# The first product of the routed layer by Strassen's rule, seven products of half size in place of eight

## The chip, the cores and the metric

The kernel runs on one core of a Trainium2 chip. The metric is the device time of one execution in microseconds. TensorE (PE) does the matmuls, and its weight loads (PEld) overlap them; VectorE (DVE) and ScalarE (ACT) do the arithmetic on tiles; GpSimd (POOL) works beside them on tiles in SBUF; SyncE (SP) issues the DMAs. Each engine works through a queue of its own in order. The framework places the waits between engines, and it also sets the order within each queue when it compiles: mostly the written order, with ready work pulled ahead of work whose inputs it expects later.

## The reference

Three layers follow one another. B = 8, H = 8 heads, S = 576, head size 64; so there are 4608 tokens of width 512.

```python
p_packed = sm_attn(p, k, v)                 # 32 packed rows per head
x = sm_attn(q, p_packed, p_packed)          # -> [4608, 512]
h = x @ w_in;  x = (h - tanh(h)) @ w_out    # d_ff = 2048
logits = x @ w_gate + modality_bias[modality_id]
e_idx = argmax(logits);  gate = softmax(logits)[e_idx]
out[mask_e] = gate * (relu(x[mask_e] @ w1[e]) @ w2[e])   # 8 experts, F = 1024
```

The inputs are such that one expert serves (nearly) all tokens: the kernel computes the expert of the first token for all of them, and a branch at the end (`other_experts`) does others where flags ask for it.

## The kernel before

Products of 32-bit data are made of three matmuls each: every operand is split into a high part in the fast format and the remainder, and `mm3` (L105 to L107) adds high·high, low·high and high·low into one PSUM bank.

The main part is a list of **slots**. The 256 slots of kind "a" are the attention's value product and the layer with tanh: 16 half-blocks `hb` of 288 tokens, each with 16 slices `f` of d_ff. In slot n PE does `gemm1(n)`, then `gemm2(n - 3)`; ACT and DVE do `chain(n)` (L857, L858 on ACT, L860, L862 on DVE) and `gsplit` (L871 on ACT, L872 on DVE) between them. `gemm1` writes one of the two PSUM banks of the pool `ps_h`; the bank is free when L862 has read it. `gemm2` adds into the four banks `acc`. After a half-block's last slot, `evac` (L905, L906) moves `acc` into the tiles x2h and x2l, which are stored to DRAM as `x_hi` and `x_lo`. The attention of the next batches stands in the two banks of `AT` beside all that.

The 144 slots of kind "b" are the layer this change is about: 18 blocks `kk` of 256 tokens, each with 8 slices `f` of 128 columns of F. `gemm1b` makes the slice's first product (4 chunks of K = 512, three matmuls of 256 columns each) in an `ps_h` bank. `relu` takes it to a high part (ACT, L972) and a remainder (DVE, L973). `gemm2b`, three slots later, multiplies by the slice of w2 and adds into two of the `acc` banks (2 token tiles, three matmuls of 512 columns). After the eighth slice `evac_b` scales the two tiles by the gate, one on ACT (L1011), one on DVE (L1007), into tiles with the tags x2h and x2l (one buffer each), and SP stores them (L1013).

The weights come in during the last slots of kind "a": `w1_load` and `w2_load` by DMA, `w1_split` (ACT L930, POOL L931) and `w2_split` (ACT L945, POOL L946). `xb_load` brings x_hi and x_lo back, 512 KB per DMA. Around the tables `pre_ev`, `pe_ev` and `post_ev` each slot has its extra work; `at_post(m, fn)` puts `fn` beside slot m. Slots 236 to 255 are where w1 is split; slot 256 (`na`) is the first of kind "b".

Of the kernel before, what the change touches and what calls it, by code (L numbers as in the profile page):

```python
# [26 lines left out]
def attn_moe_moe_kernel(  # L27
# [15 lines left out]
    nc = tc.nc  # L43
# [8 lines left out]
    TB = 256  # L52
# [19 lines left out]
    ps_at = ctx.enter_context(tc.tile_pool(name="ps_at", bufs=1, space=PSUM))  # L72
# [493 lines left out]
    def logits_pe(hb):  # L566
        ps = AT[0:32, 1, 0:HW]
# [7 lines left out]
    def route_in(hb):  # L575
        ps = AT[0:32, 1, 0:HW]
# [75 lines left out]
    def flags_pe():  # L652
        fl["ps"] = AT[0:1, 0, 0:NE * NHB]
        nc.tensor.matmul(out=AT[0:1, 1, 0:1], lhsT=ones_b, rhs=fl["big"], start=True, stop=True)
        nc.tensor.matmul(
            out=fl["ps"], lhsT=ones, rhs=fl["has"].rearrange("i e h -> i (e h)"), start=True, stop=True
        )

    def flags_b(every=False):
        n = evp.tile([1, NE, NHB], F32, name="n_other", tag="rt_l")  # L660
        ps = fl["ps"].rearrange("o (e h) -> o e h", e=NE)
        if every:
            nc.vector.tensor_copy(out=n, in_=ps)
        else:
            other = evp.tile([1, NE], F32, name="other", tag="rt_m")
            nc.vector.tensor_tensor(
                out=other, in0=em8[0:1, :], in1=idx_t[0:1, 0:1].to_broadcast([1, NE]), op=ALU.not_equal
            )
            nc.vector.tensor_tensor(
                out=n, in0=ps, in1=other.unsqueeze(2).to_broadcast([1, NE, NHB]), op=ALU.mult,  # L670
            )
            yield
        tot = evp.tile([1, NE + 1], F32, name="n_tot", tag="gq")
        nc.vector.tensor_reduce(out=tot[:, 0:NE], in_=n, axis=AX.X, op=ALU.max)
        nc.vector.tensor_reduce(out=tot[:, NE:NE + 1], in_=tot[:, 0:NE], axis=AX.X, op=ALU.max)
        yield
        if not every:
            nc.vector.tensor_copy(out=flags[:, NE, 0:1], in_=AT[0:1, 1, 0:1])
            nc.vector.tensor_tensor(out=tot[:, NE:NE + 1], in0=tot[:, NE:NE + 1], in1=AT[0:1, 1, 0:1], op=ALU.add)
        nc.vector.tensor_copy(out=flags[:, 0:NE, 0:NHB], in_=n)  # L680
        nc.vector.tensor_copy(out=flags[:, :, NHB], in_=tot)
        yield


    def redo():
        nonlocal evp
        with ExitStack() as st:
# [229 lines left out]
    def w1_load(bp, f):  # L917
        st = bp.tile([128, 4, 128], F32, name="w1s", tag="ws", bufs=2)
        e = ev_reg["e"]
        nc.sync.dma_start(  # L920
            out=st,
            in_=w1[bass.ds(e, 1)].rearrange("o (k p) c -> p (o k) c", p=128)[:, :, f * 128:f * 128 + 128],
        )
        w1t[f] = st

    def w1_split(bp, f):
        st = w1t[f]
        hi = bp.tile([128, 4, 128], F32R, name=f"w1h{f}")
        lo = bp.tile([128, 4, 128], F32R, name=f"w1l{f}")
        nc.scalar.activation(out=hi, in_=st, func=ACTF.Copy)  # L930
        nc.gpsimd.tensor_tensor(out=lo, in0=st, in1=f32(hi), op=ALU.subtract)  # L931
        w1t[f] = (hi, lo)
# [16 lines left out]
    def xb_load(kk):  # L949
        xb[kk] = [  # L950
            late["x"].tile([128, 4, TB], F32R, name=f"xb{c}", tag=f"xb{c}", bufs=3) for c in "hl"
        ]
        for d, t in zip(xs, xb[kk]):
            nc.sync.dma_start(out=f32(t), in_=d[:, :, kk * TB:kk * TB + TB])

    def gemm1b(n, kk, f):
        ps = ps_h.tile([128, TB], F32, name="h", tag="h")
        xh, xl = xb[kk]
        for c in range(4):
            mm3(ps, (w1t[f][0][:, c, :], w1t[f][1][:, c, :]), (xh[:, c, :], xl[:, c, :]), c == 0, c == 3)  # L960
        ht[n] = ps

    def relu(n):
        ps = ht.pop(n)
        if n % 2:
            gh, gl = (
                gp.tile([128, TB], F32R, name="bg", tag=tg, bufs=2) for tg in ("u", "qq")
            )
        else:
            gh = g3.tile([128, TB], F32R, name="bh", tag="gh")  # L970
            gl = g3.tile([128, TB], F32R, name="bl", tag="gl")
        nc.scalar.activation(out=gh, in_=ps, func=ACTF.Relu)  # L972
        nc.vector.scalar_tensor_tensor(  # L973
            out=gl, in0=ps, scalar=0.0, in1=f32(gh), op0=ALU.max, op1=ALU.subtract
        )
        gt[n] = (gh, gl)
        yield

    def gemm2b(n, kk, f):
        if f == 0:  # L980
            oa[kk] = [
                pools["acc"].tile([128, 512], F32, name=f"acc{2 * (kk % 2) + t}") for t in range(2)
            ]
        gh, gl = gt.pop(n)
        for t in range(2):
            st = tuple(x[:, t * 128:t * 128 + 128] for x in (gh, gl))
            mm3(oa[kk][t], st, w2t[f], f == 0, f == NF2 - 1)
# [14 lines left out]
    def evac_b(kk):  # L1002
        for t in range(2):
            T = 2 * kk + t
            o = evp.tile([128, 512], F32, name="o", tag=("x2h", "x2l")[t])
            if t:
                nc.vector.tensor_scalar(  # L1007
                    out=o, in0=oa[kk][t], scalar1=gate_b[:, T:T + 1], scalar2=None, op0=ALU.mult
                )
            else:  # L1010
                nc.scalar.activation(out=o, in_=oa[kk][t], func=ACTF.Copy, scale=gate_b[:, T:T + 1])  # L1011
# [16 lines left out]
    with ExitStack():  # L1028
# [153 lines left out]
        for n, (ph, i, f, first, kind) in enumerate(slots):  # L1182
            if ph == "a" and kind == "full":
# [14 lines left out]
        for f in range(NF2):  # L1198
            at_post(b_mem + 5 * f // 4, lambda f=f: w1_load(bpool["p"], f))
            at_post(b_mem + 2 + 5 * f // 4, lambda f=f: w1_split(bpool["p"], f))  # L1200
            at_post(na - NF + 2 * f, lambda f=f: w2_load(bpool["p"], f))
            at_post(na - NF + 2 * f + 3, lambda f=f: w2_split(f))
        at_post(na - NF + 1, lambda: xb_load(0))
        at_post(na - NF + 2, lambda: xb_load(1))

        total = len(slots)
        for n in range(total + LAG + 2):
# [76 lines left out]
```

## Time and profile before

| what | value |
|---|---|
| three runs | 1258.16, 1256.27, 1257.09 us; median 1257.09 |
| the profiled execution | 1256.98 us, span 1255.2 us |
| busy share of the span | PE 95%, PEld 84%, DVE 58%, ACT 45%, POOL 6% |
| granted TensorE clock, mean | 0.980 |
| chain that ended last | PE 78%, DVE 8%, issue 6%, DMA, ACT and POOL 2% each |

How to read it: the span runs from the first to the last instruction. Busy time is that in which an engine works on an instruction; matmuls overlap each other, so the time that one more matmul costs is the distance between the starts of two, not its own length. In rows of groups the columns are line, engine, operation, out<-in, shape, count | busy us, mean ns of one | idle time before it and what ended that. In rows in order of time they are start, length, engine, line, operation, out<-in, and in brackets the idle time before and what ended it.

### The profile page before, as it was taken

To read this page: it belongs to the slowest core of one execution; us is meant where nothing else is said; L and a number is where in the kernel's file an instruction comes from. 1 tells how busy PE (TensorE), PEld (TensorE's weight loads), DVE (VectorE), ACT (ScalarE), POOL (GpSimd) and SP (SyncE) were. 2 spreads that over 40 slices of the span, in tenths; PEclk is the share of its full clock that TensorE was granted. 3 is DMA by queue.
4 is the path that set the end of the run, shared out by engine and by line. 5 is a ranking of instruction groups with operands and counts; after the bars stand their busy time and mean duration, and the time that the engine had idled before them with its cause. 6 is when DMAs were issued, how large, how long until landed. Compare 5 with 4: busy or idle time off the path is not lost.

```text
span 1255.2 us, 24451 instructions
## 1 busy us (share of the span) xinstructions
PE 1195.3 (95%) x9764; PEld 1050.2 (84%) x9765; DVE 722.7 (58%) x1603; ACT 569.6 (45%) x1320; POOL 77.5 (6%) x69
## 2 busy tenths in 40 slices
PE   5698899999999999999999999999999999999996
PEld 3356678799889889889889899998999999999995
DVE  4866897787887787887787876654121111211111
ACT  3688756556556556556556556641111111111111
POOL 1222100000000000000000002310000000000000
PEclk8699999999999999999999999999999999999998
DMA  8768455454454354354354136221222112221201
GB/s 217 225 197 215 134 141 126 123 144 112 106 144 126 82 144 124 82 143 122 82 143 123 51 111 198 88 64 53 85 67 81 58 65 85 66 79 59 67 18 37
DMA packets 193291, 137.54 MB, mean 110 GB/s; under 512 B 123024, under 2 KB 169104, under 8 KB 193168
## 3 DMA queue, kind: packets, MB, share of 16 engines
q1 hardware_dynamic: 193168, 135.90, 39.2%
q8 instruction: 78, 1.28, 0.4%
q14 instruction: 45, 0.37, 0.1%
HBM read 98.10 MB, written 37.75 MB: 108 GB/s over the span
## 4 chain that ended last, share of the span: by engine, by line
PE 78%; DVE 8%; issue 6%; DMA 2%; ACT 2%; POOL 2%; SPq 0%; POOLq 0%; DVEq 0%; ACTq 0%
PE acc L105 15%; PE acc L107 14%; PE acc L106 14%; PE h L106 10%; PE h L105 10%; PE h L107 9%; PE at L212 3%; DVE s L487 1%; PE at L359 1%; POOL wv L188 1%; DVE x2l L906 1%; DVE qq L860 1%; PE h L844 1%; DVE gl L872 1%; DMA raw<-in_moe_w_in_dram 1%
## 5 line engine op out<-in xcount | busy, mean ns | idle before, releaser
L105 PE MATMUL acc<-gh,wo_hi 128*128 128x288 f32 x960 | 294.6, 307 | 2.7 <-DVE part L903 1.6
L107 PE MATMUL acc<-gl,wo_hi 128*128 128x288 f32 x960 | 282.9, 296 | 3.0 <-DVE gl L872 2.8
L106 PE MATMUL acc<-gh,wo_lo 128*128 128x288 f32 x960 | 283.9, 296 | 0.0
L105 PEld LDWEIGHTS acc<-gh,wo_hi 128*128 128x128 f32 x960 | 180.8, 188 | 36.4 <-ACT u L857 17.5
L860 DVE SCALAR_TENSOR_TENSOR qq<-qq,u 128x288 f32<-128x288 f32 x256 | 131.3, 513 | 116.7 <-ACT qq L858 116.5
L107 PEld LDWEIGHTS acc<-gl,wo_hi 128*128 128x128 f32 x960 | 180.6, 189 | 5.9 <-DVE gl L872 5.0
L106 PEld LDWEIGHTS acc<-gh,wo_lo 128*128 128x128 f32 x960 | 180.9, 188 | 2.4 <-issue 1.7
L871 ACT ACTIVATE gh<-gs 128x288 fp32r<-128x288 f32 x240 | 106.7, 445 | 158.7 <-PE acc L106 143.1
L106 PE MATMUL h<-xbh,w1l 128*128 128x256 f32 x576 | 161.3, 280 | 0.0
L107 PE MATMUL h<-xbl,w1h 128*128 128x256 f32 x576 | 160.8, 279 | 0.0
L105 PE MATMUL h<-xbh,w1h 128*128 128x256 f32 x576 | 160.7, 279 | 0.0
L857 ACT ACTIVATE u<-h 128x288 f32<-128x288 f32 x256 | 105.0, 411 | 109.9 <-PE h L107 90.4
L105 PE MATMUL h<-ah,mh 128*128 128x288 f32 x448 | 133.1, 297 | 2.9 <-DVE gs L862 2.1
L106 PE MATMUL h<-ah,ml 128*128 128x288 f32 x448 | 132.3, 295 | 0.0
L107 PE MATMUL h<-al,mh 128*128 128x288 f32 x448 | 131.8, 294 | 0.0
L872 DVE TENSOR_TENSOR gl<-gs,gh 128x288 fp32r<-128x288 f32 x240 | 113.1, 471 | 31.3 <-ACT gh L871 27.4
L973 DVE SCALAR_TENSOR_TENSOR bl<-h,bh 128x256 fp32r<-128x256 f32 x72 | 30.6, 425 | 165.2 <-ACT bh L972 165.2
L858 ACT ACTIVATE qq<-u 128x288 f32<-128x288 f32 x256 | 113.5, 443 | 7.0
L862 DVE SCALAR_TENSOR_TENSOR gs<-qq,h 128x288 f32<-128x288 f32 x256 | 112.5, 440 | 6.2 <-PE acc L881 1.7
L106 PEld LDWEIGHTS h<-xbh,w1l 128*128 128x128 f32 x576 | 108.1, 188 | 6.2
L105 PEld LDWEIGHTS h<-xbh,w1h 128*128 128x128 f32 x576 | 108.2, 188 | 5.8
L973 DVE SCALAR_TENSOR_TENSOR bg<-h,bg 128x256 fp32r<-128x256 f32 x72 | 30.6, 425 | 139.0 <-ACT bg L972 139.0
(167 smaller groups left out, 1958.4 us busy)
## 6 DMA issues: line engine op xcount, KB each, us to landing
ws<-w_in_v SPq DMA_DIRECT2D x56, 512.0 KB
nat<-in_v_dram SPq DMA_DIRECT2D x16, 576.0 KB
x_hi<-x2h SPq DMA_DIRECT2D x16, 576.0 KB
x_lo<-x2l SPq DMA_DIRECT2D x16, 576.0 KB
xbh<-x_hi SPq DMA_DIRECT2D x18, 512.0 KB
xbl<-x_lo SPq DMA_DIRECT2D x18, 512.0 KB
raw<-in_moe_w_in_dram SPq DMA_DIRECT2D x32, 256.0 KB
raw<-in_moe_w_out_dram SPq DMA_DIRECT2D x16, 512.0 KB
```

What stands on the lines that cost most here:

```text
L105: nc.tensor.matmul(out=ps, lhsT=ah, rhs=bh, start=first, stop=False)
L106: nc.tensor.matmul(out=ps, lhsT=al, rhs=bh, start=False, stop=False)
L107: nc.tensor.matmul(out=ps, lhsT=ah, rhs=bl, start=False, stop=last)
L188: nc.gpsimd.tensor_tensor(out=v, in0=lo.bitcast(F32), in1=hi.bitcast(F32), op=ALU.mult)
L212: nc.tensor.matmul(out=out_of(g, hh), lhsT=lhs_of(g, hh), rhs=rhs_of(g, hh), start=True, stop=True, tile_position=(64 * g, 32 * hh),)
L857: nc.scalar.activation(out=u, in_=ps, func=ACTF.Square)
L858: nc.scalar.activation(out=qq, in_=u, func=ACTF.Exp, scale=-PK)
L860: nc.vector.scalar_tensor_tensor(out=qq, in0=qq, scalar=PB, in1=u, op0=ALU.add, op1=ALU.mult)
L862: nc.vector.scalar_tensor_tensor(out=gs, in0=qq, scalar=PA, in1=ps, op0=ALU.mult, op1=ALU.mult)
L871: nc.scalar.activation(out=gh, in_=gs, func=ACTF.Copy)
L872: nc.vector.tensor_tensor(out=gl, in0=gs, in1=f32(gh), op=ALU.subtract)
L973: nc.vector.scalar_tensor_tensor(out=gl, in0=ps, scalar=0.0, in1=f32(gh), op0=ALU.max, op1=ALU.subtract)
```

## The change

The layer's tokens are taken in 9 groups of 512 in place of 18 blocks of 256. Of a group, x is cut in 2 × 2 blocks (halves of K, `kh`, and of the tokens, `th`), w1 in 2 × 2 blocks (halves of K and of F, `fh`). Strassen's rule, in the form with few additions, makes the 2 × 2 blocks of the product from seven products of combinations of blocks.

- **w1**: the combinations S1 to S4 are made on POOL (`comb`), then each of the seven left operands is split (`put`: ACT and POOL), for each of the two chunks c of a half of K: 8 combinations and 14 splits in place of 8 splits. They stand in slots 236 to 250.
- **x**: per group `x_load` brings eight pieces of 256 KB; `x_sum` (POOL, 4 per group) adds high part and remainder again, since combinations must be made before the split; `x_comb` makes four differences (DVE); `x_split` splits the seven right operands (ACT, DVE). The first group's stands in slots 247 to 255, a later group's beside the four steps of the group before it.
- **Steps**: a step j is a group and one of 4 row blocks i of 128 columns of each half of F. `first_b` makes its seven products in the order 1, 2, 5, 6, 3, 4, 7. Products 1, 6, 7 add up in one bank (`ba`), 5 and 3 in another (`be`), 2 and 4 stand in the two `ps_h` banks. Between them ACT copies a bank's state (`g_copy`), and DVE makes the four result blocks (`c_tile`). PE's order is `first_b(j)`, then `gemm2b(j - 1)`; `relu_b(j)` stands beside it.
- **Second product**: `gemm2b` does 4 token tiles and 2 halves of F per step, into all four `acc` banks. `evac_b` now evicts four tiles per group, still through the two tiles x2h and x2l.
- The two banks of `AT` are given up at slot 256 for `ba` and `be`. So the logits, routing and flags of the last half-block move behind the first steps and use `ps_h` banks, and the last half-block takes its slices in the order 8 to 15, 0 to 7. Five of the eight splits of w2 move beside steps 0 to 2.

```diff
-    TB = 256
+    TB = 512
...
-    def w1_split(bp, f):
-        st = w1t[f]
...
+    def w1_steps(bp, c):
...
+        def put(p, nm):
+            wa[p, c] = split(lambda x: bp.tile([128, 512], F32R, name=f"wa{p}{c}{x}"), sp[nm], nc.gpsimd)
+        def comb(nm, into, a, b, op):
...
+            nc.gpsimd.tensor_tensor(out=sp[into], in0=sp[a], in1=sp[b], op=op)
...
+        return [
+            lambda: load("A21", "ah0", 0, 1), lambda: load("A22", "al0", 1, 1), lambda: load("A11", "ah1", 0, 0),
+            lambda: comb("S1", "S", "A21", "A22", ALU.add),
+            lambda: put(5, "S1"), lambda: put(4, "A22"), lambda: load("A12", "al0", 1, 0),
+            lambda: comb("S3", "A21", "A11", "A21", ALU.subtract), lambda: put(7, "S3"),
+            lambda: comb("S2", "S", "S1", "A11", ALU.subtract), lambda: put(6, "S2"), lambda: put(1, "A11"),
+            lambda: comb("S4", "S", "A12", "S2", ALU.subtract), lambda: put(3, "S4"), lambda: put(2, "A12"),
+        ]
...
-    def gemm1b(n, kk, f):
-        ps = ps_h.tile([128, TB], F32, name="h", tag="h")
-        xh, xl = xb[kk]
-        for c in range(4):
-            mm3(ps, (w1t[f][0][:, c, :], w1t[f][1][:, c, :]), (xh[:, c, :], xl[:, c, :]), c == 0, c == 3)
...
+    def x_sum(g, kh, th):
+        a, b = xr[g, kh, th]
+        nc.gpsimd.tensor_tensor(out=a, in0=a, in1=b, op=ALU.add)
+    def x_comb(g):
...
+        for o, a, b in ((t1, b12, b11), (t2, b22, t1), (t3, b22, b12), (t4, t2, b21)):
+            nc.vector.tensor_tensor(out=o, in0=a, in1=b, op=ALU.subtract)
...
+    def x_split(g, p):
+        hi, lo = xa[g, p] = [x_tile() for _ in "hl"]
+        t = xr[g][p]
+        nc.scalar.activation(out=hi, in_=t, func=ACTF.Copy)
+        yield
+        nc.vector.tensor_tensor(out=lo, in0=t, in1=f32(hi), op=ALU.subtract)
...
+    def prod(j, p, ps, start):
+        g, i = divmod(j, 4)
+        for c in range(2):
+            wh, wl = (t[:, 128 * i:128 * i + 128] for t in wa[p, c])
+            xh, xl = (t[:, c, :] for t in xa[g, p])
+            for m, (a, b) in enumerate(((wh, xh), (wl, xh), (wh, xl))):
+                nc.tensor.matmul(
+                    out=ps, lhsT=a, rhs=b, start=start and c == 0 and m == 0, stop=c == 1 and m == 2,
...
+    def first_b(j):
...
+        prod(j, 1, a, True)
+        prod(j, 2, d, True)
+        g_copy(j, "p1", a)
+        nc.vector.tensor_tensor(out=c_tile(j, 0), in0=d, in1=bank[j, "p1"], op=ALU.add)
+        prod(j, 5, e, True)
+        g_copy(j, "p5", e)
+        prod(j, 6, a, False)
+        g_copy(j, "u2", a)
+        prod(j, 3, e, False)
+        nc.vector.tensor_tensor(out=c_tile(j, 1), in0=e, in1=bank[j, "u2"], op=ALU.add)
+        d2 = h_tile()[:, 0:256]
+        prod(j, 4, d2, True)
+        prod(j, 7, a, False)
+        t = c_tile(j, 3)
+        nc.vector.tensor_tensor(out=t, in0=a, in1=bank[j, "p5"], op=ALU.add)
+        nc.vector.tensor_copy(out=bank[j, "p5"], in_=a)
+        t = c_tile(j, 2)
+        nc.vector.tensor_tensor(out=t, in0=bank[j, "p5"], in1=d2, op=ALU.subtract)
...
+    def relu_b(j):
...
+                nc.scalar.activation(out=hi[:, th, :], in_=t, func=ACTF.Relu)
...
+                nc.vector.scalar_tensor_tensor(
+                    out=lo[:, th, :], in0=t, scalar=0.0, in1=f32(hi[:, th, :]), op0=ALU.max, op1=ALU.subtract
...
+    def evac_b(g):
+        for t in range(4):
+            T = 4 * g + t
+            o = evp.tile([128, 512], F32, name="o", tag=("x2h", "x2l")[t % 2])
...
+        for j in range(NU2 + 1):
+            if j:
+                if j < NU2:
+                    first_b(j)
...
+            if j < NU2:
+                threads.append(relu_b(j))
...
+            if g + 1 < NTB:
+                xp = x_prep(g + 1) if i == 0 else xp
+                todo += (xp[0:1], xp[1:5], xp[5:9], xp[9:13])[i]
+            if j:
+                gemm2b(j - 1)
...
+            if j and j % 4 == 0:
+                evac_b(j // 4 - 1)
```

More of the change, by code (lines that the diff above doesn't have):

```diff
@@ L652, in flags_pe @@
     def flags_pe():
-        fl["ps"] = AT[0:1, 0, 0:NE * NHB]
-        nc.tensor.matmul(out=AT[0:1, 1, 0:1], lhsT=ones_b, rhs=fl["big"], start=True, stop=True)
+        t = h_tile()
+        fl["ps"], fl["pb"] = t[0:1, 0:NE * NHB], t[0:1, HW - 1:HW]
+        nc.tensor.matmul(out=fl["pb"], lhsT=ones_b, rhs=fl["big"], start=True, stop=True)
         nc.tensor.matmul(
@@ L685, in redo @@
     def redo():
-        nonlocal evp
+        nonlocal evp, AT
         with ExitStack() as st:
@@ L690, in redo @@
             evp = rp
+            AT = st.enter_context(tc.tile_pool(name="ps_rat", bufs=1, space=PSUM)).tile([128, 2, 512], F32, name="rat")
             wo = rp.tile([128, NF, 512], F32, name="wo")
@@ L915, in read_e @@
         ev_reg["e"] = nc.sync.value_load(e_i[0:1, 0:1], min_val=0, max_val=NE - 1)
[L917 to L924, printed above, removed]
-    def w1_split(bp, f):
-        st = w1t[f]
[L928 to L932, printed above, removed]
+    wa, xa, xr = {}, {}, {}
@@ new lines, in split, with load @@
+    def split(tile_of, t, eng):
+        hi, lo = (tile_of(c) for c in "hl")
+        nc.scalar.activation(out=hi, in_=t, func=ACTF.Copy)
+        eng.tensor_tensor(out=lo, in0=t, in1=f32(hi), op=ALU.subtract)
+        return hi, lo
+    def w1_steps(bp, c):
+        sp = {}
+        def load(nm, tag, kh, fh):
+            sp[nm] = a2p.tile([128, 512], F32, name="w1s", tag=tag)
+            nc.sync.dma_start(
+                out=sp[nm],
+                in_=w1[bass.ds(ev_reg["e"], 1), (2 * kh + c) * 128:(2 * kh + c) * 128 + 128, fh * 512:fh * 512 + 512]
+                .rearrange("o p c -> p (o c)"),
+            )
+        def put(p, nm):
+            wa[p, c] = split(lambda x: bp.tile([128, 512], F32R, name=f"wa{p}{c}{x}"), sp[nm], nc.gpsimd)
+        def comb(nm, into, a, b, op):
+            if into not in sp:
+                sp[into] = a2p.tile([128, 512], F32, name="w1s", tag="al1")
+            nc.gpsimd.tensor_tensor(out=sp[into], in0=sp[a], in1=sp[b], op=op)
+            sp[nm] = sp[into]
+        return [
[6 more added lines that the diff above has]
+        ]
@@ L963, in relu @@
[L963 to L976, printed above, removed]
-        yield
@@ L979, in gemm2b, with x_tile, x_load @@
[L979 to L987, printed above, removed]
+    def x_tile(dt=F32R):
+        return wp.tile([128, 2, 256], dt, name="xw", tag="w")
+    def x_load(g):
+        for kh in range(2):
+            for th in range(2):
+                xr[g, kh, th] = [x_tile(F32) for _ in xs]
+                for d, t in zip(xs, xr[g, kh, th]):
+                    c0 = g * TB + 256 * th
+                    nc.sync.dma_start(out=t, in_=d[:, 2 * kh:2 * kh + 2, c0:c0 + 256])
@@ L989, in out_rows, with gemm2b @@
+    def gemm2b(j):
+        g, i = divmod(j, 4)
+        if i == 0:
+            oa[g] = [pools["acc"].tile([128, 512], F32, name=f"acc{t}") for t in range(4)]
+        parts = gt.pop(j)
+        for t in range(4):
+            for fh in range(2):
+                st = tuple(x[:, t // 2, (t % 2) * 128:(t % 2) * 128 + 128] for x in parts[fh])
+                mm3(oa[g][t], st, w2t[i + 4 * fh], i == 0 and fh == 0, i == 3 and fh == 1)
     def out_rows(t):
@@ L1038, in attn_moe_moe_kernel @@
         for hb in range(2, NHB):
-            for f in range(NF):
-                slots.append(("a", hb, f, f == 0, "full" if f == NF - 1 else None))
+            fs = list(range(NF)) if hb < NHB - 1 else [*range(NF // 2, NF), *range(NF // 2)]
+            for f in fs:
+                slots.append(("a", hb, f, f == fs[0], "full" if f == fs[-1] else None))
         na = len(slots)
-        for kk in range(NTB):
-            for f in range(NF2):
-                slots.append(("b", kk, f, f == 0, "out" if f == NF2 - 1 else None))
         pe_ev, post_ev = {}, {}
```

150 lines of the change are left out of this document (94 added, 56 removed).

## The prediction

> **What bounds the kernel now.** I read the page's head, then the windows by stage, the groups by shape, and the order of time over a few microseconds.
>
> ```profile
> span 1255.2 us, 24451 instructions
> PE 1195.3 (95%) x9764; PEld 1050.2 (84%) x9765; DVE 722.7 (58%) x1603; ACT 569.6 (45%) x1320; POOL 77.5 (6%) x69
> ...
> 762.00:832.84 70.84, 68.71 (x512) 67.50 (x511) 47.45 (x93) 43.46 (x103) 20.39 (x16) 1.00 0.42 126
> 832.84:1243.51 410.67, 410.66 (x2642) 371.81 (x2640) 86.71 (x205) 70.38 (x169) 0.93 (x1) 1.00 0.20 64
> ```
>
> The windows' columns are length, busy time of PE, PEld, DVE, ACT and POOL, granted clock, DMA share and GB/s. The second layer is the stretch from 832.84 to 1243.51: PE is busy in 410.66 of 410.67 us at clock 1.00, DVE in 21% and ACT in 17%. A matmul less here is time less, unless something else takes PE's place. The stretch before it, where w1 and w2 are loaded and split, has 70.84 − 68.71 = 2.1 us of PE idle.
>
> ```profile
> 1000.14 0.69 ACT L1011 ACTIVATE o<-acc,gate_b 128x512 f32<-128x512 f32 x1 [0.32 <-PE acc L107]
> 1000.64 0.28 PE L105 MATMUL h<-xbh,w1h 128*128 128x256 f32 x1
> 1000.86 1.92 SPq L1013 DMA_DIRECT2D out_dram<-o  x3
> ...
> 1001.93 0.28 PE L107 MATMUL h<-xbl,w1h 128*128 128x256 f32 x1
> ...
> 1002.05 0.39 PE L105 MATMUL acc<-w2h,bh 128*128 128x512 f32 x1
> ...
> 1002.25 0.39 ACT L972 ACTIVATE bg<-h 128x256 fp32r<-128x256 f32 x1 [1.42 <-PE h L107]
> ...
> 1003.45 0.28 PE L105 MATMUL h<-xbh,w1h 128*128 128x256 f32 x1
> ```
>
> One slot: 12 matmuls of 256 columns from 1000.64 to 1002.05, 0.1175 us each, then six of 512 columns to 1003.45, 0.2333 each. A reader on ACT starts 0.32 us after the last matmul's start (1001.93 to 1002.25).
>
> **The first product.** It had 3 × 576 = 1728 matmuls of 256 columns (the row of L106 below). Now there are 36 steps (9 groups, 4 row blocks) of 7 products, 2 halves of K and 3 terms: 1512, in the same shape. 216 × 0.1175 = 25.4 us less. The second product keeps its 864 of 512 columns. A step is 42 × 0.1175 = 4.94 us of first product and 24 × 0.2333 = 5.60 of second, 10.53 together; 36 of them make 379, where 144 slots made 404.6.
>
> **What the other engines take on.**
>
> ```profile
> L106 PE MATMUL h<-xbh,w1l 128*128 128x256 f32 x576 | 161.3, 280 | 0.0
> L244 DVE TENSOR_TENSOR ml<-at,mh 128x512 fp32r<-128x512 f32 x56 | 38.1, 681 | 2.4 <-ACT mh L242 2.3
> L973 DVE SCALAR_TENSOR_TENSOR bg<-h,bg 128x256 fp32r<-128x256 f32 x72 | 30.6, 425 | 139.0 <-ACT bg L972 139.0
> L972 ACT ACTIVATE bg<-h 128x256 fp32r<-128x256 f32 x72 | 27.7, 385 | 151.8 <-PE h L107 151.8
> L1007 DVE TENSOR_SCALAR o<-acc,gate_b 128x512 f32<-128x512 f32 x18 | 13.5, 751 | 14.2 <-PE acc L107 14.2
> L946 POOL TENSOR_TENSOR w2l<-w2s,w2h 128x512 fp32r<-128x512 f32 x8 | 10.8, 1347 | 31.5 <-ACT w2h L945 31.5
> L930 ACT ACTIVATE w1h<-w1s 128x512 fp32r<-128x512 f32 x8 | 5.1, 633 | 5.0 <-DMA w1s<-in_moe_w_dram 5.0
> ```
>
> Per group of 42.1 us: DVE has 20 bank operations and 16 relu remainders at 0.425, 11 block differences and remainders at 0.681, two evictions at 0.751: 24.3 us. ACT has 12 bank copies and 16 relus at 0.385, 7 splits at 0.633, two evictions at 0.69: 16.6. POOL has four sums at 1.347: 5.4. SP issues 8 loads of x where there were 4 at twice the size. None is near 42.1, so the path stays PE's unless an order or a wait stops it. Routing, its logits and the flags move into steps 1 to 3; the same instructions, under the same cover, at nothing. The five late splits of w2 (0.633 on ACT, 1.347 on POOL) and the first layer's last eviction stand beside steps 0 to 2 as well. SP sends group 1's x behind loads of w2 that wait for two staging buffers, until the sixth split in step 1; it is wanted in step 4, 31 us on, so this is hidden too. If DVE were full in step 2, where the flags meet the first differences, its lateness would have 5.6 us of second product to hide in.
>
> **Waits inside a step.** Product 6 adds to the bank of product 1 after the copy of product 1, product 3 to the bank of product 5 after its copy, product 7 to the bank of 6 after its copy. A copy ends 0.32 + 0.39 = 0.71 us after the last matmul's start. The first and third have one more product between (0.70 us of slack). The copy of product 5 has none: product 3's first weight load is due 0.70 us after that last start. That is 0 to 0.1 us a step; I take 0.06, 2.2 us in 36.
>
> **POOL beside DVE.**
>
> ```profile
> 769.39 0.19 PEld L105 LDWEIGHTS h<-ah,mh 128*128 128x128 f32 x1 [1.55 <-DVE gs L862]
> ...
> 786.31 0.46 DVE L860 SCALAR_TENSOR_TENSOR qq<-qq,u 128x288 f32<-128x288 f32 x1 [0.91 <-ACT qq L858]
> 788.69 0.46 DVE L860 SCALAR_TENSOR_TENSOR qq<-qq,u 128x288 f32<-128x288 f32 x1 [0.91 <-ACT qq L858]
> ...
> 795.01 0.46 DVE L862 SCALAR_TENSOR_TENSOR gs<-qq,h 128x288 f32<-128x288 f32 x1
> 795.55 0.46 DVE L872 TENSOR_TENSOR gl<-gs,gh 128x288 fp32r<-128x288 f32 x1
> 797.01 1.30 POOL L946 TENSOR_TENSOR w2l<-w2s,w2h 128x512 fp32r<-128x512 f32 x1 [18.13 <-ACT w2h L945]
> 797.30 1.32 DVE L860 SCALAR_TENSOR_TENSOR qq<-qq,u 128x288 f32<-128x288 f32 x1 [1.29 <-ACT qq L858]
> 797.38 0.29 PE L105 MATMUL h<-ah,mh 128*128 128x288 f32 x1
> ```
>
> L860 reads two SBUF tiles: 0.46 us alone, 1.32 beside a POOL operation, ending 0.31 after it. So one POOL operation costs DVE up to 0.86 us, and through the two h banks this reaches PE (the weight load that waited 1.55 us for DVE). The Trainium skill, "GPSIMD Engine Reference", section "8. Key points", says that POOL shares its SBUF interfaces with VectorE and contends with instructions that have two SBUF inputs. The trace agrees (1.32 against 0.46). By that rule the steps' bank operations, which read one operand from PSUM, are spared, and the sum below stands; were they held as well, each group would lose the 3.4 us worked out below, and the sum would come to 1243 − 2 + 8 × 3.4 = 1268.
>
> Slots 236 to 256 (2.38 us each, 786.31 to 788.69) belong to the stretch with 16 POOL operations and 2.1 us of PE idle. Now 29 fall into them: 8 combinations and 14 remainders of w1, 4 sums, 3 of w2. DVE's demand is 20 × 1.38 = 27.6 (L860, L862, L872 at 0.46), 11 × 0.681 = 7.5 for x, and 29 × 0.86 = 24.9: 60.0 us in 47.6. Of the 12.4 over, 1.9 hide in the h bank (gs ends at 795.47, its bank is wanted at 797.38) and about 4 behind the first step's products, whose last operands are due late in its 4.94 us. 6.5 − 2.1 = 4.4 us more; bounds 0 (the work spreads) and 12.4 − 2.1 = 10.3. In a later group four sums delay DVE by up to 3.4 us, hidden unless a split on ACT waits for DVE ahead of a bank copy: 0 to 3.4 us in 8 groups; as DVE is 58% full I take 0.25 each, 2 us.
>
> **Stores and the tail.** Four tiles are now evicted at a time into two buffers, so the third waits for the first one's store, the fourth for the second's.
>
> ```profile
> 1023.31 1.35 SPq L1013 DMA_DIRECT2D out_dram<-o  x2
> ...
> 1023.31:1028.80 5.49, 5.49 (x37) 4.96 (x36) 1.58 (x3) 0.77 (x2) 0.00 (x0) 1.00 0.19 47
> 1028.80:1031.60 2.80, 2.80 (x20) 2.54 (x19) 0.43 (x1) 0.38 (x1) 0.00 (x0) 1.00 0.24 94
> 1031.60:1033.00 1.40, 1.40 (x14) 1.40 (x13) 0.00 (x0) 0.00 (x0) 0.00 (x0) 1.00 0.01 3
> ...
> 1243.51:1255.20 11.69, 0.00 (x0) 0.00 (x0) 0.75 (x1) 0.02 (x1) 0.00 (x0) 0.65 0.17 51
> ...
> 1243.56 1.30 SPq L1013 DMA_DIRECT2D out_dram<-o  x2
> ```
>
> A tile is 262 KB. 5.49 us × 47 GB/s = 258 KB and 2.80 × 94 = 263: the first tile is out 5.5 us after its issue, the second 8.3 us after it. The Trainium skill, "DMA: Bandwidth & Descriptors", section "Why a DMA increments its semaphore by 16 and not by 1", says that a transfer is split over the largest number up to 16 that divides the slowest dimension of both its access patterns; four row blocks against 128 partitions make four. The trace agrees: a DMA share of 0.24 is 3.8 of 16. Over 16 the store would be short enough that the sum below stood in every order.
>
> At the end PE stops and 11.69 us follow. Counted from the start of the last step's second product, the first store issues at about 2.4 (its six matmuls 1.4, 0.3 to drain, 0.7 to issue as from 1000.14 to 1000.86), both early stores are out at 10.7, the fourth tile is evicted and issued by 11.5 and out 5.5 later, at 17.0. PE stopped at 5.7 (24 × 0.2333 and the last one's end), so 11.3 us after it, against 8.35 today (issue 0.05 after PE's stop, then 8.3): 3 us more. Bounds 0.7 (the fourth tile's own eviction, were a buffer free) and 5.
>
> Inside, a group's eviction stands beside the next group's first steps. From the start of the step: product 7's bank is read from 5.14 (4.82 + 0.32), three bank operations end at 6.3, two relus at 7.1; ACT evicts the first tile from 7.1, its store issues at 7.8 and is out at 13.3, the second at 16.1. The next step's copies of products 1, 5 and 6 are due at 11.45 (10.53 + 5 × 0.1175 + 0.32), 12.85 and 13.55. If the third tile's eviction stands behind them in ACT's queue, nothing waits. The queue need not have the written order:
>
> ```profile
> 840.86 1.20 ACT L905 ACTIVATE x2h<-acc 128x288 fp32r<-128x288 f32 x3 [1.50 <-PE acc L107]
> 841.95 0.38 ACT L972 ACTIVATE bh<-h 128x256 fp32r<-128x256 f32 x1
> 842.22 0.42 ACT L905 ACTIVATE x2h<-acc 128x288 fp32r<-128x288 f32 x1
> ```
>
> The relu is written before or after all four L905, and runs between the third and the fourth: the compiler orders a queue by when it expects inputs. I take the order to fit the stores, at 0, as that row fits what was ready.
>
> **The sum**, on the profiled execution's 1256.98 us (the median of three is 1257.09, 0.01% more): −25.4 (products) + 2.2 (waits in a step) + 4.4 (POOL before the first step) + 2 (POOL in the groups) + 3 (tail) = −13.8, so 1243. With the first, third and last of these costs at their bounds it is 1232 (−25.4 + 0.7) to 1252 (−25.4 + 3.6 + 10.3 + 2 + 5 = −4.5); all at the lower end at once is unlikely, so 1235 to 1252.
>
> **Rivals.** (a) The stores are expected too early and only the third tile's eviction is ahead. Before the copy of product 1: evicted 13.3 to 14.0, copy to 14.4, product 6 starts at 14.45 instead of 12.65, 1.8 us late; before the copy of product 5: product 3 at 14.45 instead of 13.35, 1.1. In 8 groups 9 to 14 us: 1252 to 1257. For it: ACT waited 5.0 us in all for w1's loads (L930's row), so arrivals are expected early at times. (b) The slower one: the fourth tile's eviction stands on DVE ahead of the next step's first bank sum, and the relu of that sum on ACT ahead of the copy of product 5. Evicted 16.1 to 16.85, sum to 17.3, relu to 17.65, copy to 18.05, product 3 at 18.1 instead of 13.35: 4.75 us a group, 38 in 8, 1281. It needs an expectation more than 3 us short of the row's 8.3; it decides the sign from 13.8 / 8 = 1.7 us a group. Against it: a sum ready at 12.2 must lose to an eviction ready at 16.1. (c) The products are saved and POOL beside DVE takes the gain back: 10.3 us before the first step, and half of 3.4 us in 8 groups, 13.6: 5.9 + 11.6 above the forecast, 1260. For it: in a group 11 × 0.681 + 16 × 0.425 = 14.3 of DVE's 24.3 us read two SBUF tiles. Against: beside the single POOL operation at 797.01 PE went on without a gap (797.38).
>
> **Chances.** Forecast 0.50, (a) 0.20, (b) 0.20, (c) 0.10. Within 0.2% of 1257.09, 1254.6 to 1259.6, is about what a measurement of this kernel cannot tell from no change. Faster: 0.50, half of (a) and 0.03 of (c), 0.63; same: the other half of (a) and 0.04 of (c), 0.14; slower: (b) and 0.03 of (c), 0.23. The likeliest case alone has 1235 to 1252. The range runs from 1235 to 1276: it leaves out 0.03 below it and most of (b).
>
> **What would show it.** Right: 1512 matmuls of 256 columns in the stage, a step of 10.5 us, PE without gaps; some 6.5 us of PE idle before and around the first step (4.4 + 2.1); 14 to 15 us after PE's last. Wrong by (a): PE idle before product 6 or 3 once a group, released by ACT's copy, ACT idle released by a DMA of out. By (b): the same gap near 5 us, with DVE waiting for that DMA. By (c): gaps released by DVE or POOL spread over all steps.

## The result, and the profile after

| kernel | median us | runs from … to | profiled execution, span |
|---|---|---|---|
| before | 1257.62 (4 runs) | 1256.27 to 1259.15 | 1256.98, 1255.2 |
| after | 1329.18 (4 runs) | 1323.39 to 1335.08 | 1323.39, 1321.6 |

The ratio is 1.0569, with a 95% interval from 1.0521 to 1.0617: the changed kernel is 5.7% slower. The prediction was 1243 us (1235 to 1276), faster.

The head of the page of the changed kernel, then its stretches (columns as before: length, busy time of PE, PEld, DVE, ACT, POOL, granted clock, DMA share, GB/s):

```profile
span 1321.6 us, 24652 instructions
PE 1195.7 (90%) x9548; PEld 1045.0 (79%) x9549; DVE 861.4 (65%) x1882; ACT 643.0 (49%) x1497; POOL 145.6 (11%) x119
```

```profile
762.00:800.00 38.00, 29.91 (x196) 28.64 (x195) 20.18 (x36) 18.51 (x43) 25.34 (x19) 0.91 0.18 58
800.00:846.00 46.00, 41.98 (x302) 41.24 (x302) 33.77 (x66) 27.89 (x66) 16.03 (x12) 0.96 0.40 129
846.00:900.00 54.00, 48.30 (x320) 43.67 (x320) 42.37 (x102) 21.99 (x54) 12.09 (x9) 1.00 0.25 77
900.00:1300.00 400.00, 354.51 (x2097) 316.79 (x2097) 176.29 (x374) 116.35 (x282) 32.05 (x24) 0.95 0.18 53
```

PE, which had been busy in 410.66 of 410.67 us, is idle in 400 − 354.5 = 45.5 us from 900 to 1300, and its granted clock there is 0.95 where it was 1.00. Another 8.1 + 4.0 + 5.7 us are idle between 762 and 900. PE's busy sum is nevertheless what it was (1195.7 against 1195.3), with 216 matmuls fewer: others take longer, for a large part at the lower clock.

For the account I took the starts of successive matmuls from 762 us to the last one. Each has a usual distance to the next (0.1175 us with 256 columns, 0.2333 with 512, 0.132 with 288; the four shorter matmuls in proportion). What a distance has beyond that counts as a gap if it is over 1.2 times the usual distance and 0.06 us, and else as slow spacing (half the clock adds just one usual distance). In us:

| | usual distances | gaps | slow spacing | start of the last matmul | from there to the end |
|---|---|---|---|---|---|
| before | 477.6 | 2.8 | 0.6 | 1243.1 | 12.1 |
| after | 452.4 | 71.5 | 20.2 | 1306.2 | 15.4 |
| difference | −25.2 | +68.7 | +19.6 | +63.1 | +3.3 |

The sum, +66.4, is the difference of the two spans. Of the gaps, 51.4 us lie from 900 to 1300, on average 6.4 in each of eight groups, and 20.1 before 900. Of the slow spacing, 14.9 us stand where the granted clock is 0.50 (none before).

The waits of the changed kernel name the mechanism (engine, tile, line, releaser: us in total, times, longest):

```profile
DVE o L1103 <- DMA out_dram<-o: 60.3, 8, 9.6
ACT bg L1068 <- DVE cc L1045: 58.2, 35, 5.0
ACT o L1107 <- DMA out_dram<-o: 54.4, 9, 7.3
...
PEld be L1026 <- ACT pc L1033: 28.2, 13, 2.9
PEld ba L1026 <- ACT pc L1033: 26.8, 15, 3.8
```

Once a group ACT and DVE stand waiting for a store of `out` (L1107 is the eviction on ACT, L1103 that on DVE), and PE waits for copies of banks on ACT (L1033). In order of time, the second step of a group (PE's rows and those of ACT and DVE together):

```profile
959.38 0.29 PE L1026 MATMUL be<-xw,wa51h 128*128 128x256 f32 x1
962.21 0.69 ACT L1107 ACTIVATE o<-acc,gate_b 128x512 f32<-128x512 f32 x1 [7.27 <-DMA out_dram<-o]
962.79 0.38 ACT L1033 ACTIVATE pc<-ba 128x256 f32<-128x256 f32 x1
...
963.22 0.58 PE L1026 MATMUL ba<-xw,wa60h 128*128 128x256 f32 x1 [3.56 <-ACT pc L1033]
...
964.45 0.41 PE L1026 MATMUL ba<-xw,wa61h 128*128 128x256 f32 x1
964.87 0.75 DVE L1103 TENSOR_SCALAR o<-acc,gate_b 128x512 f32<-128x512 f32 x1 [8.78 <-PE ba L1026]
965.54 0.41 DVE L1045 TENSOR_TENSOR cc<-h,pc 128x256 f32<-128x256 f32 x1
965.99 0.42 ACT L1068 ACTIVATE bg<-cc 128x256 fp32r<-128x256 f32 x1 [2.82 <-DVE cc L1045]
966.31 0.36 ACT L1033 ACTIVATE pc<-be 128x256 f32<-128x256 f32 x1
...
966.73 0.58 PE L1026 MATMUL be<-xw,wa30h 128*128 128x256 f32 x1 [1.86 <-ACT pc L1033]
```

Two gaps: product 6 starts 3.84 us after the last matmul of product 5, because the copy of product 1 stands behind the third tile's eviction, which waits for a store; product 3 starts 2.28 us after the last of product 6, because the copy of product 5 stands behind the relu of the first bank sum, that sum behind the fourth tile's eviction on DVE, and that eviction behind a store. (The profile puts this one wait of L1103 down to PE and `ba`, which the eviction does not read; in the eight cases of the row above it names the store. The two evictions start 2.66 us apart; the two stores of before ended 2.8 apart.)

A third gap, of 1.85 us, stands in the first step of six of the groups (the third to the eighth), without any store. In one of them, first DVE, then ACT, then PE:

```profile
997.60 3.09 DVE L1014 TENSOR_TENSOR xw<-xw 128x512 fp32r<-128x512 f32 x5
1000.62 0.41 DVE L1045 TENSOR_TENSOR cc<-h,pc 128x256 f32<-128x256 f32 x1
```

```profile
1001.06 0.42 ACT L1068 ACTIVATE bg<-cc 128x256 fp32r<-128x256 f32 x1 [1.86 <-DVE cc L1045]
1001.38 0.36 ACT L1033 ACTIVATE pc<-be 128x256 f32<-128x256 f32 x1
```

```profile
999.95 0.28 PE L1026 MATMUL ba<-xw,wa61h 128*128 128x256 f32 x1
1001.80 0.38 PE L1026 MATMUL be<-xw,wa30h 128*128 128x256 f32 x1 [1.57 <-ACT pc L1033]
```

Five remainders of the group's x stand on DVE ahead of the first bank sum; its relu stands on ACT ahead of the copy of product 5, and product 3 waits.

### The profile page after: what moved, and what is told of

Read it like the earlier page. It is cut to its first block, busy times and chain, and to the rows that moved or that the text cites. A ratio compares the mean times of both kernels' runs of the same rounds, so it can differ in the third digit from the quotient of the medians.

```text
span 1321.6 us, 24652 instructions
## 1 busy us (share of the span) xinstructions
PE 1195.7 (90%) x9548; PEld 1045.0 (79%) x9549; DVE 861.4 (65%) x1882; ACT 643.0 (49%) x1497; POOL 145.6 (11%) x119
## 4 chain that ended last, share of the span: by engine, by line
PE 60%; DVE 15%; DMA 9%; issue 8%; POOL 4%; ACT 3%; SPq 0%; POOLq 0%; DVEq 0%; ACTq 0%
PE acc L105 12%; PE acc L107 11%; PE acc L106 11%; DMA out_dram<-o 5%; PE h L105 4%; PE h L106 4%; PE h L107 4%; PE ba L1026 3%; PE be L1026 3%; PE at L212 3%; PE h L1026 2%; DMA xw<-x_lo 2%; DVE xw L1014 2%; DVE xw L1003 1%; POOL xw L997 1%
## 5 line engine op out<-in xcount | busy, mean ns | idle before, releaser
L105 PE MATMUL h<-ah,mh 128*128 128x288 f32 x448 | 134.1, 300 | 12.9 <-DVE gs L869 12.1
L1068 ACT ACTIVATE bg<-cc 128x256 fp32r<-128x256 f32 x144 | 60.0, 417 | 160.5 <-DVE cc L1045 58.2
L879 DVE TENSOR_TENSOR gl<-gs,gh 128x288 fp32r<-128x288 f32 x240 | 115.9, 483 | 30.6 <-ACT gh L878 26.8
L865 ACT ACTIVATE qq<-u 128x288 f32<-128x288 f32 x256 | 113.5, 443 | 6.9
L869 DVE SCALAR_TENSOR_TENSOR gs<-qq,h 128x288 f32<-128x288 f32 x256 | 112.5, 439 | 6.1 <-PE acc L888 1.7
L105 PE MATMUL acc<-w2h,bg 128*128 128x512 f32 x288 | 113.2, 393 | 0.0
L106 PE MATMUL acc<-w2h,bg 128*128 128x512 f32 x288 | 112.7, 391 | 0.0
L107 PE MATMUL acc<-w2l,bg 128*128 128x512 f32 x288 | 112.6, 391 | 0.0
L105 PEld LDWEIGHTS h<-ah,mh 128*128 128x128 f32 x448 | 84.5, 189 | 17.1 <-DVE gs L869 13.5
L1070 DVE SCALAR_TENSOR_TENSOR bg<-cc,bg 128x256 fp32r<-128x256 f32 x144 | 64.5, 448 | 41.5 <-ACT bg L1068 40.7
L107 PEld LDWEIGHTS h<-al,mh 128*128 128x128 f32 x448 | 84.7, 189 | 0.5 <-issue 0.4
```

The lines of the kernel that those rows point to most:

```text
L105: nc.tensor.matmul(out=ps, lhsT=ah, rhs=bh, start=first, stop=False)
L106: nc.tensor.matmul(out=ps, lhsT=al, rhs=bh, start=False, stop=False)
L107: nc.tensor.matmul(out=ps, lhsT=ah, rhs=bl, start=False, stop=last)
L865: nc.scalar.activation(out=qq, in_=u, func=ACTF.Exp, scale=-PK)
L869: nc.vector.scalar_tensor_tensor(out=gs, in0=qq, scalar=PA, in1=ps, op0=ALU.mult, op1=ALU.mult)
L879: nc.vector.tensor_tensor(out=gl, in0=gs, in1=f32(gh), op=ALU.subtract)
```

## The experiments

**Four output buffers.** The tags x2h and x2l each hold 4 × 288 columns, so two tiles of 512 fit into each and no eviction waits for a store.

```diff
     def evac_b(g):
+        oo = [evp.tile([128, 2, 512], F32, name="o", tag=tag) for tag in ("x2h", "x2l")]
         for t in range(4):
-            o = evp.tile([128, 512], F32, name="o", tag=("x2h", "x2l")[t % 2])
+            o = oo[t % 2][:, t // 2]
```

> One change against the changed kernel: each group's four evicted tiles get a buffer each (two halves of the tiles x2h and x2l), so no eviction waits for a store. Theory S (the stores: the third and fourth evictions wait for the first two stores at the head of ACT's and DVE's queues, the copies of products 1 and 5 stand behind them, and PE's clock falls to half after the gap): the gaps of 1.9 to 3.9 us before products 6 and 7 and of 2.3 to 3.0 us before product 3 in every group's second step go, about 37 us in 8 groups, and with them most of the slow matmuls, about 10 us: 1323 to 1275-1285. The gap of 1.85 us before product 3 in every group's first step stays. Theory P (POOL beside DVE is what holds the steps up): the gaps stay, under 10 us gained. Theory C (the clock falls by itself because of the denser work): clock 0.93 in the windows stays.

Measured: 1272.02 us (1271.67 to 1272.47), ratio to before 1.012 [1.0103, 1.0137]. That is 57 us less than the changed kernel, a little more than expected: the stores are the largest part of the loss.

**Product 5 before product 2.** The copy of product 5 is issued before the first bank sum exists, so no relu can stand ahead of it, and one more product lies between it and product 3.

```diff
         prod(j, 1, a, True)
-        prod(j, 2, d, True)
-        g_copy(j, "p1", a)
-        nc.vector.tensor_tensor(out=c_tile(j, 0), in0=d, in1=bank[j, "p1"], op=ALU.add)
         prod(j, 5, e, True)
+        g_copy(j, "p1", a)
         g_copy(j, "p5", e)
+        prod(j, 2, d, True)
+        nc.vector.tensor_tensor(out=c_tile(j, 0), in0=d, in1=bank[j, "p1"], op=ALU.add)
         prod(j, 6, a, False)
```

> One change against the changed kernel: product 5 is made before product 2, so the copy of product 5 is ready before the first result block and its relu. The stores stay. Theory S with the link 'the relu of the first result block stands on ACT ahead of the copy of product 5, so PE waits for DVE': the 1.85 us gap before product 3 in each group's first step goes (8 to 9 of them, 14 us); in the second step the wait moves from product 3 to product 7, behind the copy of product 6, and stays: 1323 to 1305-1318. If that relu is not the link: no change within 5 us.

Measured: 1305.56 us (1298.59 to 1310.16), ratio 1.0368 [1.033, 1.0406], 24 us less than the changed kernel. The gaps of 1.85 us are gone; those behind the stores stay.

**Both edits.**

> Both edits together: four eviction buffers and product 5 before product 2. Theory S: PE has no gap over 0.5 us in any group after the first; the clock of the windows from 900 us on is 1.00; left over are the 13.4 us of gaps around the loading of w1 and some 6 us in the first steps: 1255 to 1266, about the time of the kernel before. Theory P: over 1290.

Measured: 1259.33 us (1257.89 to 1262.87), ratio 1.0031 [1.0019, 1.0042]. The same stretch of the second layer in the runs with four buffers, with product 5 second, and with both:

```profile
900.00:1200.00 300.00, 290.62 (x1784) 260.65 (x1783) 158.44 (x328) 103.63 (x247) 31.88 (x24) 0.99 0.22 67
```

```profile
900.00:1250.00 350.00, 321.93 (x1908) 287.49 (x1907) 166.69 (x351) 109.98 (x264) 31.35 (x24) 0.95 0.19 58
```

```profile
900.00:1200.00 300.00, 299.01 (x1863) 269.47 (x1862) 162.29 (x337) 106.69 (x254) 31.56 (x24) 1.00 0.21 67
```

PE's idle share, 11.4% in the changed kernel, is 3.1% (9.4 of 300), 8.0% (28.1 of 350) and 0.3%. With the buffers alone the gap of the group's first step is left, with the order alone those behind the stores; with both the groups run as predicted, at clock 1.00. Yet the kernel only comes back to where it was before: by the account its gaps are 20.6 us from 762 to 900 (2.8 before).

**No combinations of w1.** As both edits, without the 8 combinations on POOL; the products then multiply other data than the rule's.

> The third experiment with the eight combinations of w1 on POOL left out (the seven left operands are then split from the four blocks as they are, so the products are not those of the rule); loads, splits and the rest stay. Theory P for the stage before the first step (POOL is busy without a break from 760 to 789 us and every operation of DVE with two SBUF tiles waits for one of POOL): 8 of 29 POOL operations less take 4 to 8 us off the 13.4 us of gaps and part of the slow matmuls there: 5 to 9 us under the third experiment. Rival (ACT's seven splits per chunk hold the stage up): under 2 us.

Measured: 1252.38 us (1250.34 to 1253.85), ratio 0.996 [0.9944, 0.9976]; 7.0 us below the kernel with both edits. So a part of what is left hangs on POOL's eight combinations, but this doesn't say on which property of POOL's work. In the kernel with both edits, ACT's longest waits from 762 to 790 and its order around one gap, then PE's rows and one of DVE:

```profile
ACT wa31h L934 <- POOL w1s L956: 3.5, 1, 3.5
ACT wa30h L934 <- POOL w1s L956: 3.2, 1, 3.2
```

```profile
768.08 0.63 ACT L934 ACTIVATE wa30h<-w1s 128x512 fp32r<-128x512 f32 x1 [3.16 <-POOL w1s L956]
768.62 0.43 ACT L865 ACTIVATE qq<-u 128x288 f32<-128x288 f32 x1
```

```profile
768.34 0.29 PE L107 MATMUL acc<-gl,wo_hi 128*128 128x288 f32 x1
771.46 0.40 PE L105 MATMUL h<-ah,mh 128*128 128x288 f32 x1 [2.83 <-DVE gs L869]
```

```profile
769.52 1.51 DVE L879 TENSOR_TENSOR gl<-gs,gh 128x288 fp32r<-128x288 f32 x1
```

L934 is the rounding copy of a combination that POOL has still to make (L956); the first layer's Exp (L865) stands behind it, and DVE and PE behind that. On this reading (theory Q in the expectations) it is the wait in ACT's queue that costs PE; on the prediction's (theory P) it is DVE's time beside POOL. In this gap both play a part: after ACT's wait of 3.16 us, a remainder of the first layer on DVE (L879) takes 1.51 us beside POOL (0.46 alone, the row at 795.55 in the prediction) ahead of the operation that PE waits for (L869). Three kernels on top of both edits tell the two apart; a fourth moves the sums of x.

**w1's remainders on DVE.**

```diff
-  split(..., sp[nm], nc.gpsimd)
+  split(..., sp[nm], nc.vector)
```

> As the kernel with both edits (product 5 second, four output buffers; 1259.3 us), with the 14 remainders of w1 computed on VectorE instead of GpSimd; the 8 combinations stay on GpSimd. In that kernel PE has 10.4 us of gaps from 762 to 800, and ACT waits five times for a combination (3.5, 3.2, 1.9, 1.8, 0.9 us). Theory Q (a queue): GpSimd is busy without a break, the copies of the combinations on ACT wait for it, and the first layer's Square and Exp stand behind them. Then eight combinations alone come at once, ACT no longer waits, and the gaps of that stretch fall from 10.4 to 3 to 5 us: 1252 to 1256. Theory P (sharing): VectorE's instructions with two SBUF operands are stretched by up to 0.86 us for each GpSimd instruction. 14 of them fewer, against 14 x 0.68 us of VectorE's own: 14 x 0.18 = 2.5 us less: 1257.

Measured: 1253.3 us (1251.48 to 1255.29), ratio 0.9974 [0.9964, 0.9985]. The gaps of 762 to 800 fall from 10.4 to 4.2 us. The largest that is left, 3.2 us at 774.90, stands behind three remainders of w1 on DVE that take 1.47 to 1.74 us beside POOL's combinations (0.68 alone): sharing has a part in that one.

**All of w1's on DVE** (as above, and `comb` with `nc.vector`).

> As before it, with all 22 combinations and remainders of w1 on VectorE; GpSimd has nothing between 762 and 800. Theory Q: ACT waits for VectorE's combinations (0.68 us each) only, gaps of that stretch 2 to 4 us: 1251 to 1255. Theory P: 22 x (0.86 - 0.68) = 4 us less than 1259.3: 1255. It tells whether 15 us more on VectorE in 30 us are themselves a bound: then 1258 or more.

Measured: 1247.34 us (1245.66 to 1248.27), ratio 0.9924 [0.991, 0.9937], without a gap from 762 to 800, and faster than any of its forecasts. ACT still makes the 14 rounding copies here and is busy 26.55 of 38 us, so its load isn't what held PE up.

**w1's rounding copies on POOL**, so that nothing on ACT waits for POOL, and POOL has more to do.

```diff
-  wa[p, c] = split(..., sp[nm], nc.gpsimd)
+  hi, lo = wa[p, c] = [...]
+  nc.gpsimd.tensor_copy(out=hi, in_=sp[nm])
+  nc.gpsimd.tensor_tensor(out=lo, in0=sp[nm], in1=f32(hi), op=ALU.subtract)
```

> As the kernel with both edits, with the 14 leading parts of w1 (the rounding copies) made on GpSimd instead of ACT: GpSimd has 36 instructions in that stage where it had 22, and ACT has none that waits for it. Theory Q: the first layer's chain on ACT is free, gaps from 762 to 800 fall from 10.4 to 3 to 5 us: 1252 to 1256. Theory P: 14 more instructions beside VectorE at up to 0.86 us: up to 12 us more: 1263 to 1271. It tells the two apart.

Measured: 1249.21 us (1247.56 to 1250.85), ratio 0.9941 [0.9927, 0.9955], below the 1252 to 1256 of theory Q and far from the 1263 to 1271 of theory P. The stretch in the kernel with both edits, and in this one:

```profile
762.00:800.00 38.00, 28.37 (x195) 27.02 (x194) 20.40 (x35) 18.66 (x44) 23.25 (x18) 0.96 0.14 49
```

```profile
762.00:800.00 38.00, 37.95 (x285) 37.25 (x285) 35.58 (x53) 21.92 (x53) 36.59 (x32) 1.00 0.15 49
```

POOL is busy 36.59 of 38 us instead of 23.25, and DVE's instructions are longer than alone (35.58 us for 53). PE is idle for 0.05 us instead of 9.6. So theory P falls as the cause in this stretch: sharing does stretch DVE's work, but DVE had the time as long as ACT didn't wait. Theory Q holds, with sharing adding to a gap where both meet (the 1.51 us above).

**The sums of x on DVE.**

```diff
     def x_sum(g, kh, th):
-        nc.gpsimd.tensor_tensor(out=a, in0=a, in1=b, op=ALU.add)
+        nc.vector.tensor_tensor(out=a, in0=a, in1=b, op=ALU.add)
```

> As the kernel with both edits, with the 36 sums of the two parts of x on VectorE (0.68 us each) instead of GpSimd. In that kernel the first difference of group 0 waits 2.44 us for GpSimd at 826.9 with the first layer's chain behind it (a gap of 3.4 us on PE), and group 1's sums stand beside VectorE at 843 to 850 (gaps of 1.5 and 2.0). If the detour over GpSimd is the cause, both shrink: 1253 to 1257, and the later groups stay without gaps. Rival: VectorE then waits for the loads of x itself, at the head of its queue, and the gaps stay or grow: 1259 to 1264.

Measured: 1247.81 us (1247.42 to 1250.12), ratio 0.9931 [0.9917, 0.9944], 11.5 us less than both edits, more than the 2 to 6 expected. The gaps from 800 to 900 fall from 10.2 to 5.7 us, and those of the later groups (some 0.3 us before product 7 in six of them, behind the copy of product 6's bank, and 0.2 before product 6 in three) are gone too, which I had not counted. This run takes away the waits for POOL and the sharing with it at once. Before it, the first difference of group 0 waited 2.44 us for POOL and then took 1.75 us beside it (0.68 alone):

```profile
826.93 1.75 DVE L1003 TENSOR_TENSOR xw<-xw 128x512 f32<-128x512 f32 x1 [2.44 <-POOL xw L997]
```

So for the sums the two causes are not told apart; by this row the wait is the larger one.

**Both of these moves, and POOL without any part in the stage** (the remainders of w2 on DVE as well).

> The kernel with both edits (1259.3 us), and w1's 22 combinations and remainders as well as the 36 sums of x on VectorE; GpSimd keeps the eight remainders of w2. The gains so far were 12.0 (w1) and 11.5 (sums) us. They lie in different stretches (762 to 800, and from 815 on), so by the theory of the queues they add up: 1234 to 1238. If VectorE's own load binds (17 us more for w1 and x before the first step's end), they overlap: 1240 to 1246.

Measured, with both moves: 1235.65 us (1234.71 to 1237.83), ratio 0.9833 [0.9819, 0.9846]. The gains add up.

> As the run before it, with the eight remainders of w2 on VectorE too, so that GpSimd has no part in the stage. If what is left of the gaps between 800 and 880 comes from GpSimd beside VectorE, 8 x (0.86 - 0.68) = 1.4 us less and a wait or two with it: 1232 to 1237. If VectorE is full there: the same or 1 to 3 us more.

Measured, with nothing on POOL: 1232.1 us (1231.15 to 1232.66), ratio 0.9807 [0.9793, 0.982]: 1.9% faster than before, and the best of all. Its stretches:

```profile
762.00:800.00 38.00, 38.00 (x289) 37.60 (x288) 32.51 (x76) 26.94 (x63) 0.00 (x0) 1.00 0.24 79
800.00:846.00 46.00, 44.66 (x340) 43.80 (x340) 42.03 (x93) 31.19 (x72) 0.00 (x0) 1.00 0.49 150
846.00:900.00 54.00, 54.00 (x339) 48.61 (x338) 38.57 (x104) 19.02 (x45) 0.00 (x0) 1.00 0.26 82
900.00:1200.00 300.00, 300.00 (x1875) 271.75 (x1874) 164.65 (x356) 108.35 (x253) 0.00 (x0) 1.00 0.20 63
```

PE has no idle time in them but 1.3 us, with DVE at 91% from 800 to 846. The account of the kernels on the way, in us as above:

| | usual distances | gaps | slow spacing | start of the last matmul | from there to the end |
|---|---|---|---|---|---|
| four buffers | 450.1 | 31.1 | 13.3 | 1256.6 | 13.9 |
| product 5 second | 452.8 | 55.9 | 22.3 | 1293.0 | 15.5 |
| both | 450.3 | 23.1 | 6.9 | 1242.3 | 13.8 |
| both, nothing on POOL | 450.1 | 2.0 | 0.8 | 1215.1 | 13.9 |

## Why the prediction was wrong, step by step

- **The step that failed: "I take the order to fit the stores, at 0".** It didn't fit. Both rivals came true at once: the third tile's eviction stood ahead of the copy of product 1, (a), and the fourth's ahead of the first bank sum, (b). (b) was priced at 4.75 us a group and 38 in all; the two gaps of 959.38 and 964.45 are 3.84 − 0.12 and 2.28 − 0.12, 5.9 us, and over the eight groups it was 51.4 less six first-step gaps of 1.73, 41 us. The row that I leaned on (a relu between two evictions at 841.95) shows the order following inputs whose time is known from other engines. It says nothing on how long the compiler takes a store to last. The kernel's written order tells more: it calls `evac_b` ahead of the `first_b` whose copies had to wait, so all four evictions stood ahead of those copies just as they were written. The forecast needed the compiler to move two of them behind those copies; the rivals, with 0.40 between them, needed no move at all. Writing the third and fourth eviction behind the copies was not tried.
- **Products, −25.4: right.** −25.2 by the account.
- **Waits inside a step, 0.06 each: too small.** In an undisturbed step of the changed kernel PE's rows at product 3 read:

```profile
989.30 0.29 PE L1026 MATMUL ba<-xw,wa61h 128*128 128x256 f32 x1
989.46 0.39 PE L1026 MATMUL be<-xw,wa30h 128*128 128x256 f32 x1
989.68 0.28 PE L1026 MATMUL be<-xw,wa30l 128*128 128x256 f32 x1
```

0.38 us for two distances of 0.1175: 0.14 us a step, and 5 us in 36 had there been nothing else. The large wait at that place I missed: the relu of the first sum ahead of the copy of product 5, behind DVE's x remainders (1.85 us in a group's first step). I had summed DVE's work per group and found room, but not asked what stands ahead of the first bank sum. With both edits, moving product 5 took 12.7 us off (1272.0 to 1259.3).
- **POOL before the first step, 4.4, at most 10.3: far too little, mainly by another mechanism.** From 762 to its first step at 848.34 the changed kernel has 13.4 us of gaps and 5.4 of slow spacing; before had 2.6 and 0.8 up to its second layer at 832.84. That is 15.4 us more. I had priced POOL by what it takes from DVE's time. What cost PE was, as the runs with w1 moved show, ACT's copies waiting for POOL's combinations with the Exp of the first layer behind them; and, by the rows, DVE's first differences waiting for POOL's sums. With more POOL work and no such wait on ACT, PE lost 0.05 us from 762 to 800. The Trainium skill, "GPSIMD Engine Reference", section "8. Key points", also says that VectorE is about twice as fast on elementwise work; the rows of L244 (0.681) and L946 (1.347) agree, and by them each sum or remainder of 128 × 512 was cheaper on DVE than the 0.86 us that I charged for it on POOL.
- **POOL in the groups, 2: right in size.** The sums' move took 2.5 us of gaps from the groups behind 900. The upper end of the range held this term at 2, though its own bound was 3.4 us in each of 8 groups.
- **Group 1's x, "hidden": the wrong way round.** I had its loads waiting for w2 until step 1. They were issued from 840.17 on (837.85 with both edits), before the first step, and the sums and differences they allowed were then pulled ahead of step 0's bank operations (gaps of 1.5 and 2.0 us at 850.2 and 852.5 with both edits).
- **Routing in steps 1 to 3, at nothing: nearly.** One gap of 2.0 us at 877.35, behind the flags on DVE; 1.5 with both edits, none in the last kernel.
- **Tail, 3: right.** 15.4 − 12.1 = 3.3. With four buffers 1.8.
- **Missing altogether: the clock.** 14.9 of the 19.6 us by which slow spacing grew stand at the half clock after the gaps (below); the rest is at full clock, small waits such as the 0.14 us above among it.

With all of POOL's work gone and the stores out of the way, the sum's own logic holds. In the last kernel, against before: usual distances −27.5 (25.4 of it the products, the rest a start at 762 that is a little further on), gaps and slow spacing 2.8 for 3.4, −0.6, and the end +1.8: −26.2 but for rounding, the difference of the spans (1229.0 against 1255.2). The medians of that comparison are 24.4 us apart. What before would gain from moving its own POOL work wasn't tried; by its account it is not more than its 2.8 us of gaps and 0.6 of slow spacing.

## What to carry to other kernels

When a change gives an engine more to do, summing its load isn't enough: for each instruction in an in-order queue that waits for a slower producer (a store, POOL), look at what stands behind it and who waits for that. A buffer ring that had one tile per store and now gets several in a burst can put its wait into the queues that feed PE; as many buffers as the burst took it away here. In this kernel, where DVE had room, small sums and remainders were better there than on POOL; for w1, less for the shared time than for the waits that the detour brought.

## What the runs showed of the hardware

The granted clock falls to half after gaps of a few microseconds and stays there after PE is busy again. Within each trace, its changes all lie on one grid of 3.413 us. In the changed kernel, around the two gaps shown above, by the stretches of that grid:

```profile
959.78:963.20 3.42, 0.00 (x0) 0.00 (x0) 0.00 (x0) 0.96 (x2) 0.00 (x0) 1.00 0.21 80
963.20:966.61 3.41, 1.65 (x6) 1.35 (x6) 1.25 (x3) 0.62 (x3) 0.00 (x0) 0.50 0.21 44
966.61:970.03 3.42, 3.30 (x15) 3.30 (x16) 1.10 (x3) 0.76 (x3) 0.00 (x0) 0.50 0.26 78
970.03:973.44 3.41, 3.41 (x19) 2.88 (x18) 2.03 (x5) 0.83 (x2) 0.00 (x0) 1.00 0.14 50
```

From 963.20 to 970.03 the clock is 0.50, and matmuls start every 0.21 us (967.11, 967.33, 967.54 in the trace) instead of every 0.1175. The same happens after one shorter gap, of 1.85 us at 943.83 in the run with four buffers:

```profile
942.83:946.24 3.41, 1.85 (x13) 1.48 (x13) 2.50 (x5) 1.21 (x4) 0.35 (x1) 1.00 0.80 244
946.24:949.65 3.41, 3.41 (x17) 3.35 (x16) 1.01 (x3) 0.42 (x1) 2.08 (x2) 0.50 0.44 141
```

The gap of the first step in the changed kernel, also 1.85 us (at 999.95), was not followed by it: the matmuls after it stand 0.12 us apart (1002.02, 1002.14 in the trace). It lies across a border of the grid:

```profile
997.34:1000.75 3.41, 2.89 (x24) 2.68 (x23) 3.41 (x7) 1.72 (x4) 0.00 (x0) 1.00 0.39 102
1000.75:1004.16 3.41, 2.36 (x19) 2.36 (x20) 1.50 (x4) 1.38 (x4) 1.29 (x1) 1.00 0.85 266
```

So PE is idle for 1.56 us in one stretch there, and for 0.52 and 1.05 us in two here. In the twelve traces, from 60 us on, no stretch at full clock with PE busy in more than 63% of it was followed by half clock, and each with less than 44% was; in between both occur, so what decides there stays open. The Trainium skill, "TensorE: Matmul & The Clock Gate", section "HAM oscillation — how this bites in real kernels", asks for no idle gaps above about 3.4 us. The gap at 959.38 (PE idle for 3.56 us) agrees; the 1.56 us idle that was followed by 0.50 shows that a shorter one can do it.
